# Block sums of the second output matrix formed from the float32 weights, one group's x sums moved to VectorE, and another order of the last output products

## The chip, the cores and the metric

One core of a Trainium2 chip runs the whole program. The metric is the device time of one execution in microseconds, the median of several runs. The engines are called as in the profile: PE (TensorE matmuls), PEld (its weight loads), DVE (VectorE), ACT (ScalarE), POOL (GpSimd), SP (SyncE, whose queue issues most DMAs).

## The reference

Attention with a relative bias over 4 x 8 heads of 576 x 64, then two feed-forward layers over 2304 tokens of 512 features. The change concerns the second layer:

```python
def _moe2_ref(x, w_gate, w_val, w_out):        # x 2304 x 512, d_ff 1536
    gate = 1.0 / (1.0 + np.exp(-(x @ w_gate)))
    val = x @ w_val
    return (gate * val @ w_out).astype(np.float32)
```

## The kernel before

Every float32 operand is split into two f16 parts, high and low, and a product is three f16 matmuls (high by high, high by low, low by high). The weights are decoded from their raw words (`decode`, L186), scaled and split in place: `w2f[mat]` (L1157) holds matrix `mat` (0 gate, 1 value, 2 output) as float32 and, after `w2_split` (L1179), as f16 pairs over the same memory (`w2h16`).

The second layer works on 18 tiles of 128 tokens in five groups of 4, 2, 4, 4 and 4 tiles (`sizes`). Groups 0 and 1 use plain products: `gate_val` (L1398) for gate and value, `second_out` (L1627) for the output. Groups 2 to 4 use a scheme of seven block products in place of eight for each 2 x 2 block product. This scheme needs sums of blocks on both sides:

- `w2_sums` (L1309) forms them for gate and value weights, on DVE with copies by ACT, into tiles `w2s`. There is one set for each of three parts `jc` of the 1536 inner features.
- `x2_sums` (L1338) forms x's sums of group 2 into tiles `x2s0` to `x2s3`, which have one buffer each. For groups 3 and 4, `next_sums` (L1424) forms x's sums one half `t` at a time in the tile `xx` (one buffer), stores them in DRAM (`xt_d`), and `load_sums` (L1455) loads them again.
- `out_sums` (L1483) forms the output matrix's sums from the f16 pairs of `w2h16[2]`: ten additions, three copies and three subtractions per `jc`, into `w3s`. For `jc` 0 and 1 DVE adds and ACT copies; for `jc` 2 POOL does both. `out_first` (L1497) forms the remaining sum, in place of the block b12, with four DVE operations and one ACT copy per `jc`. All of this runs when group 2 begins: `out_sums` for 0, 2, 1 and `out_first(0)` ahead of the loop at L1686, the other two `out_first` behind the first `gate7` of group 2.

`gate7` (L1514) makes 14 products of 12 matmuls for one `jc` (seven for the gate, seven for the value, by `seven`, L1381) and from them seven f16 pieces `ap`. Its float32 results take ten tiles of the ring `fr`. `out7` (L1594) makes the seven products of the output for one `jc` into four accumulators `c11`, `c12`, `c21`, `c22`; `out_last` (L1565) does it for the last `jc` of the last group and stores the blocks. Products go to eight PSUM buffers `prod`. `add` (L1300) is an operation by DVE and `padd` (L1440) one by POOL.

The loop over g = 2, 3, 4 has this order: `gate7(0)`, then x's sums for the next group, `gate7(1)`, `out7(0)`, `gate7(2)`, `load_sums`, `out7(1)`, `out7(2)` or `out_last`. The sums of group 3 are halved: t = 0 by DVE, t = 1 by POOL; both halves of group 4 are POOL's.

The order of instructions on each engine is set ahead of the run by a scheduler that goes by priority (the order of the program text, unless raised) and simulated readiness; `tc.issue_after(i)` puts what follows behind the instruction `i`. The weight work of the second layer is a list of small steps, `units` (L1223 to L1230), each with a count; `take(n)` (L1233) hands out n counts of them between the steps of attention's end and of `gate_val` for group 0 (5 per step for j below 8, then 7). Each engine and each DMA queue works in its order.

Of the kernel before, what the change touches and what calls it, by code (L numbers as in the profile page):

```python
# [102 lines left out]
def attn_moe_kernel(  # L103
# [19 lines left out]
    x2_d = dram.tile([18, 128, 4, 2, 128], F16, name="x2_d")  # L123
    xt_d = dram.tile([2, 2, 128, 2, 4, 2, 128], F16, name="xt_d")
# [592 lines left out]
    def split_w(w, s_, hi, lo, tmp, scaler=None, sub=None):  # L717
# [5 lines left out]
        (sub or pool).tensor_tensor(out=lo, in0=tmp, in1=hi, op=ALU.subtract)  # L723
# [498 lines left out]

    steps = [(m, jc) for jc in range(3) for m in range(2)]  # L1223
# [4 lines left out]
    units += decs(2, 0) + decs(2, 1) + decs(2, 2)  # L1228
    units += [(1, lambda: urgent(w2_scale_out))]
    units += [(1, lambda jc=jc, c=c: w2_split(2, jc, c)) for jc in range(3) for c in range(4)]  # L1230
    given = [0, 0]
# [208 lines left out]
    def padd(out_, a, b, op=ALU.add):  # L1440
        glob["pool"] = pool.tensor_tensor(out=out_, in0=a, in1=b, op=op)  # L1441

# [37 lines left out]
    def phigh(x, dst):  # L1480
        pool.tensor_scalar(out=dst(0), in0=x, scalar1=1.0, scalar2=None, op0=ALU.mult)

    def out_sums(jc, plus, top, tmp):  # L1483
        b11, b21, b12, b22 = out_blocks(jc)
        st_ = w3_p.tile([128, 3, 2, 2, 256], F16, name=f"w3s{jc}")

        def part(n):
            return lambda l, kk=None: st_[:, n, l] if kk is None else st_[:, n, l, kk]
        t2, t3, t4 = (part(n) for n in range(3))
        u, x, y, v = (tmp(n) for n in range(4))  # L1490
        tsums(u, x, y, v, b11, b21, b12, b22, plus)
        for f, dst_ in ((x, t2), (y, t3), (v, t4)):
            top(f, dst_)
            plus(dst_(1), f, dst_(0), ALU.subtract)
        osum[jc] = dict(b11=b11, b21=b21, b22=b22, t1=b12, t2=t2, t3=t3, t4=t4)

    def out_first(jc, plus, top):  # L1497
        w = osum[jc]
        u, v = ctile(0), ctile(3)
        plus(u, w["t1"](0), w["b11"](0), ALU.subtract)  # L1500
        plus(v, w["t1"](1), w["b11"](1), ALU.subtract)
        plus(u, u, v)
        top(u, w["t1"])
        plus(w["t1"](1), u, w["t1"](0), ALU.subtract)
# [45 lines left out]
    def put(g, th, e, c, tts):  # L1550
        o = slice(256 * e, 256 * e + 256)
        for tt in tts:
            tl = tiles[first[g] + 2 * th + tt]
            if tl[0] == "D":
                _, bp, qd, b, r = tl
                r0 = (2 * bp + b) * S + 256 * qd
                sp.dma_start(out=out[r0:r0 + 256, o].rearrange("(p r) m -> r p m", r=2)[r], in_=c[:, tt])
# [128 lines left out]
    for g in range(2, 5):  # L1686
        p0 = gate7(0, xs_)
        if g == 2:
            out_first(1, add, high)
            out_first(2, add, high)  # L1690
# [83 lines left out]
```

## Time and profile before

| | |
|---|---|
| median of three runs | 1057.43 us (1053.62 to 1063.36) |
| profiled execution, its own time | 1061.63 us |
| its span in the trace | 1059.8 us |
| busy, PE / PEld / DVE / ACT / POOL | 894.4 / 669.8 / 817.9 / 673.4 / 565.6 us |

The trace is of one execution on the chip; its times count from the span's start. A line such as L1301 can be that of a helper (`add`), so tiles say more than lines. PE's ends are modelled, so a piece of twelve matmuls reads 1.47 us where the next starts after 1.31. An engine's wait is put down to the last thing that it waited for.

### The profile page before, as it was taken

The numbers are of one execution on the slowest core, as the hardware profiler recorded it, in microseconds if no ns is written. First come the engines' busy times: TensorE is split into PE (matmuls) and PEld (weight loads), VectorE is DVE, ScalarE is ACT, GpSimd is POOL, SyncE is SP. The second block draws the span as 40 slices with busy tenths as digits, with TensorE's granted clock in tenths as the row PEclk, the third lists the DMA queues.
The fourth block names the chain that finished last, engine by engine and source line by source line (L and its number), as shares of the span: only waits on it lengthen the run. The fifth ranks groups of instructions, "written<-read, shape, count | busy, mean of one in ns | idle before, by whom it ended". The sixth has DMA issues, their size and how long they took to land. (4 is left out here: it accounts for less than half of the span.)

```text
span 1059.8 us, 25088 instructions
## 1 busy us (share of the span) xinstructions
PE 894.4 (84%) x9944; PEld 669.8 (63%) x9944; DVE 817.9 (77%) x1568; ACT 673.4 (64%) x1337; POOL 565.6 (53%) x514
## 2 busy tenths in 40 slices
PE   2646665678888799999998789999997889999997
PEld 2524454455666666677685465455766778888886
DVE  6879899786666766667568877589999966877877
ACT  4789886758677787888868976864333433443432
POOL 3357556565665556546642577230063575786346
PEclk9756565689999899999999989999999999999999
DMA  7878999899999999899878335010010131013001
GB/s 223 283 243 209 236 249 243 219 215 197 192 184 199 173 200 185 169 226 196 160 179 308 128 130 199 1 40 31 11 40 1 41 103 49 2 62 106 5 2 40
DMA packets 263046, 150.42 MB, mean 142 GB/s; under 512 B 216976, under 2 KB 237968, under 8 KB 262928
## 3 DMA queue, kind: packets, MB, share of 16 engines
q1 hardware_dynamic: 259632, 145.67, 57.1%
q0 software_dynamic: 2048, 1.58, 0.6%
q8 instruction: 78, 1.28, 0.5%
q10 hardware_dynamic: 1248, 1.57, 0.4%
q14 instruction: 40, 0.33, 0.1%
HBM read 84.03 MB, written 22.28 MB: 100 GB/s over the span
## 5 line engine op out<-in xcount | busy, mean ns | idle before, releaser
L617 POOL TENSOR_TENSOR p<-p,p 128x1024 f16<-128x1024 f32 x72 | 158.4, 2200 | 124.4 <-ACT p L616 84.1
L605 ACT ACTIVATE p<-p,m,sc 128x576 f32<-128x576 f32 x144 | 123.9, 863 | 2.4
L1301 DVE TENSOR_TENSOR fr<-prod,fr 128x512 f32<-128x512 f32 x144 | 95.4, 685 | 29.8 <-ACT fr L1385 15.6
L598 DVE CUSTOM_DVE_ANT_0 p<-score,gk 128x576 f32<-128x576 f32 x144 | 102.9, 750 | 11.0 <-PE score L580 7.1
L847 PE MATMUL x2ps<-lt,w1f 128*128 128x128 f16 x1728 | 108.1, 223 | 3.4 <-ACT lt L835 1.9
L847 PEld LDWEIGHTS <-w1f 128*128 128x128 f16 x1728 | 103.4, 100 | 4.0 <-issue 1.8
L1413 PE MATMUL s_ps<-xb,w2f 128*128 128x512 f16 (+1 forms) x576 | 99.3, 330 | 6.0 <-DVE fr L1419 4.8
L641 PE MATMUL xps<-gk,pt 128*128 128x64 f16 (+1 forms) x2240 | 86.8, 202 | 12.4 <-DMA pt<-p 10.7
L1377 PEld LDWEIGHTS <-w2f 128*128 128x128 f16 x864 | 85.5, 99 | 17.9 <-issue 7.1
L1441 POOL TENSOR_TENSOR ap<-fr,ap 128x512 f16<-128x512 f32 x45 | 59.0, 1322 | 69.7 <-ACT ap L1510 69.7
L641 PEld LDWEIGHTS <-pt 128*128 128x128 f16 (+1 forms) x2240 | 81.8, 106 | 22.7 <-DMA pt<-p 13.1
L464 PEld LDWEIGHTS <-mask 128*128 128x128 f16 (+1 forms) x1312 | 61.8, 118 | 53.9 <-issue 24.3
L1510 ACT ACTIVATE ap<-fr 128x512 f16<-128x512 f32 x63 | 38.9, 628 | 81.4 <-DVE fr L1521 46.1
L1413 PEld LDWEIGHTS <-w2f 128*128 128x128 f16 x576 | 56.4, 99 | 48.1 <-issue 10.3
L790 PE MATMUL hps<-w1f,xt 128*128 128x512 f16 x312 | 78.5, 399 | 5.7 <-DVE gk L263 3.0
L1542 PEld LDWEIGHTS <-ap 128*128 128x128 f16 x756 | 74.0, 98 | 8.6
L1377 PEld LDWEIGHTS <-w2s 128*128 128x128 f16 x648 | 64.6, 100 | 19.2 <-issue 10.5
L575 PE MATMUL score<-gk,qt 64*128 64x512 f16 x384 | 59.6, 416 | 17.8 <-DVE m L598 9.3
L464 PE MATMUL bp<-rhs,mask 128*128 128x64 f16 (+1 forms) x960 | 49.4, 219 | 28.7 <-DVE gb L490 11.3
L790 PEld LDWEIGHTS <-xt 128*128 128x128 f16 x384 | 37.8, 101 | 48.5 <-issue 13.5
L616 ACT ACTIVATE p<-p 128x1152 f16<-128x1152 f32 x54 | 62.4, 1158 | 9.1 <-DMA pt<-p 7.0
L1377 PE MATMUL prod<-x2s,w2s 128*128 128x256 f16 x432 | 55.6, 280 | 8.7 <-ACT fr L1385 8.7
(244 smaller groups left out, 2139.2 us busy)
## 6 DMA issues: line engine op xcount, KB each, us to landing
gk<-bias_d SPq DMA_DIRECT2D x24, 576.0 KB
wraw<-in_moe_w_out_dram SPq DMA_DIRECT2D x20, 512.0 KB
sraw<-in_q_dram SPq DMA_DIRECT2D x12, 384.0 KB
sraw<-in_k_dram SPq DMA_DIRECT2D x12, 384.0 KB
sraw<-in_v_dram SPq DMA_DIRECT2D x12, 384.0 KB
bias_d<-gk SPq DMA_DIRECT2D x8, 576.0 KB
qraw<-in_q_dram SPq DMA_DIRECT2D x64, 64.0 KB
kv<-in_k_dram SPq DMA_DIRECT2D x32, 128.0 KB
```

The costliest lines, as they stand in the source:

```text
L464: pe.matmul(big[0:np_, jj // 8, o:o + 64], lhsT, rhs[i].rearrange("p c h g -> p (c h g)"), start=(i == 0), stop=(i == 1),)
L598: dve.tensor_tensor_reduce(out=pp[:, hh], in0=score[:, 960 * hh:960 * hh + S], in1=bi, scale=1.0, scalar=-3.0e38, op0=ALU.add, op1=ALU.max ...
L605: act.activation(out=pp[:, hh], in_=pp[:, hh], func=ACTF.Exp, bias=m[:, 2 + hh:3 + hh], scale=col(C), accum_out=sm[:, c + hh:c + hh + 1])
L616: act.activation(out=hi, in_=pp, func=ACTF.Copy)
L617: pool.tensor_tensor(out=p16[:, :, 640:1152], in0=view(pp, 0, [[640, 2], [1, 512]]), in1=view(p16, 0, [[1280, 2], [1, 512]]), op=ALU.subtract)
L641: pe.matmul(o, a, b_, start=(n == 0), stop=(n == len(seq) - 1))
L790: pe.matmul(h, xt[:, xl, kk, off:off + 128], win16[:, 2 * kk + n, wl], start=(kk == 0 and xl == 0 and wl == 0), stop=(kk == 3 and xl == 1),)
L847: pe.matmul(ps[:, dc], wout16[:, f, wl, 128 * dc:128 * dc + 128], lt[:, ll, f], start=(n == 0), stop=(n == 23))
L1301: glob["dve"] = dve.tensor_tensor(out=out_, in0=a, in1=b, op=op)
L1377: pe.matmul(p[:, jf, 0:nn], w(wl, kk, jf), x(xl, kk), start=(m == 0), stop=(m == 5))
L1413: pe.matmul(ps[:, 0:n], w[:, 4 * (j // 4) + c, wl, o:o + 128], xx[:, 0:n, c, xl, :], start=(m == 0), stop=(m == 11))
L1542: pe.matmul(p[:, tt], a[:, al, kk, 128 * tt:128 * tt + 128], w(wl, kk), start=(m == 0), stop=(m == 5))
```

## The change

The sums of the output matrix are formed from the float32 weights as soon as these are decoded, before the in-place split overwrites them: four float32 subtractions by POOL per `jc` (`out_adds`), into temporaries that lie in the tiles of the `w2s` sums for `jc` 1 and 2. Behind the last split, ACT scales and rounds them, POOL forms the low parts (`out_split`), and SP stores the pairs in DRAM (`to_d`), by way of the tiles `x2s0` to `x2s3`. When group 2 begins, `out_sums` loads them, three sums into `w3s` and one over the block b12. `out_first` and `phigh` are gone. Both halves of x's sums of group 3 are DVE's. `out_last` makes its products in another order, adds with DVE where POOL did twice, and its stores alternate between SP and ACT.

```diff
@@ -121,6 +121,7 @@
     dram = enter(ctx, "scratch", 1, space=DRAM)
     bias_d = dram.tile([5, 128, H, 640], F32, name="bias_d")
     x2_d = dram.tile([18, 128, 4, 2, 128], F16, name="x2_d")
+    to_d = dram.tile([3, 128, 4, 2, 2, 256], F16, name="to_d")
     xt_d = dram.tile([2, 2, 128, 2, 4, 2, 128], F16, name="xt_d")
 
     const = enter(ctx, "const")
@@ -720,7 +721,7 @@
         else:
             pool.tensor_scalar(out=tmp, in0=w, scalar1=s_, scalar2=0.0, op0=ALU.mult, op1=ALU.add)
         act.activation(out=hi, in_=tmp, func=ACTF.Copy)
-        (sub or pool).tensor_tensor(out=lo, in0=tmp, in1=hi, op=ALU.subtract)
+        glob["split"] = (sub or pool).tensor_tensor(out=lo, in0=tmp, in1=hi, op=ALU.subtract)
 
     def behind(f):
         with tc.issue_after(glob["qk"].ins):
@@ -1220,14 +1221,46 @@
     def scale(m, jc):
         return [(1, lambda: urgent(lambda: (w2_scale_gate, w2_scale_val)[m](jc)))]
 
+    def padd(out_, a, b, op=ALU.add):
+        glob["pool"] = pool.tensor_tensor(out=out_, in0=a, in1=b, op=op)
+
+    tmps = {}
+
+    def out_adds(jc):
+        if jc == 0:
+            four = [sw_p.tile([128, 3, 2, 256], F32, name=f"w2s{m}{n}") for n in (1, 2) for m in range(2)]
+            tmps.update((n, four[n // 3][:, n % 3]) for n in range(12))
+        b11, b21, b12, b22 = (w2f[2][:, 4 * jc + 2 * kh:4 * jc + 2 * kh + 2, 256 * e:256 * e + 256]
+                              for kh, e in ((0, 0), (1, 0), (0, 1), (1, 1)))
+        u, x, y, v = (tmps[4 * jc + n] for n in range(4))
+        padd(u, b12, b11, ALU.subtract)
+        padd(x, b22, u, ALU.subtract)
+        padd(y, b22, b12, ALU.subtract)
+        padd(v, b21, x, ALU.subtract)
+
+    def behind_splits(jc):
+        with tc.issue_after(glob["split"].ins):
+            out_split(jc)
+
+    def out_split(jc):
+        for n in range(4):
+            f = tmps[4 * jc + n]
+            d = xs_p.tile([128, 2, 2, 256], F16, name=f"x2s{n}")
+            act.activation(out=f, in_=f, func=ACTF.Copy, scale=sw[:, jc, S_O:S_O + 1])
+            act.activation(out=d[:, 0], in_=f, func=ACTF.Copy)
+            padd(d[:, 1], f, d[:, 0], ALU.subtract)
+            sp.dma_start(out=to_d[jc, :, n], in_=d)
+
     steps = [(m, jc) for jc in range(3) for m in range(2)]
     units = decs(*steps[0])
     for n, (m, jc) in enumerate(steps):
         units += decs(*steps[n + 1]) if n < 5 else []
         units += scale(m, jc) + splits(m, jc)
-    units += decs(2, 0) + decs(2, 1) + decs(2, 2)
+    for jc in range(3):
+        units += decs(2, jc) + [(1, lambda jc=jc: out_adds(jc))]
     units += [(1, lambda: urgent(w2_scale_out))]
     units += [(1, lambda jc=jc, c=c: w2_split(2, jc, c)) for jc in range(3) for c in range(4)]
+    units += [(1, lambda jc=jc: behind_splits(jc)) for jc in range(3)]
     given = [0, 0]
 
     def take(n):
@@ -1437,9 +1470,6 @@
             plus(dst_(1), f, dst_(0), ALU.subtract)
         sp.dma_start(out=xt_d[g - 3, t], in_=xx)
 
-    def padd(out_, a, b, op=ALU.add):
-        glob["pool"] = pool.tensor_tensor(out=out_, in0=a, in1=b, op=op)
-
     def tsums(u, x, y, v, b11, b21, b12, b22, plus):
         plus(u, b12(0), b11(0), ALU.subtract)
         plus(v, b12(1), b11(1), ALU.subtract)
@@ -1477,31 +1507,16 @@
     def ctile(n):
         return c_p.tile([128, 2, 256], F32, name=f"c{n}")
 
-    def phigh(x, dst):
-        pool.tensor_scalar(out=dst(0), in0=x, scalar1=1.0, scalar2=None, op0=ALU.mult)
-
-    def out_sums(jc, plus, top, tmp):
+    def out_sums(jc):
         b11, b21, b12, b22 = out_blocks(jc)
         st_ = w3_p.tile([128, 3, 2, 2, 256], F16, name=f"w3s{jc}")
+        sp.dma_start(out=st_, in_=to_d[jc, :, 1:4])
+        for l in range(2):
+            sp.dma_start(out=b12(l), in_=to_d[jc, :, 0, l])
 
         def part(n):
             return lambda l, kk=None: st_[:, n, l] if kk is None else st_[:, n, l, kk]
-        t2, t3, t4 = (part(n) for n in range(3))
-        u, x, y, v = (tmp(n) for n in range(4))
-        tsums(u, x, y, v, b11, b21, b12, b22, plus)
-        for f, dst_ in ((x, t2), (y, t3), (v, t4)):
-            top(f, dst_)
-            plus(dst_(1), f, dst_(0), ALU.subtract)
-        osum[jc] = dict(b11=b11, b21=b21, b22=b22, t1=b12, t2=t2, t3=t3, t4=t4)
-
-    def out_first(jc, plus, top):
-        w = osum[jc]
-        u, v = ctile(0), ctile(3)
-        plus(u, w["t1"](0), w["b11"](0), ALU.subtract)
-        plus(v, w["t1"](1), w["b11"](1), ALU.subtract)
-        plus(u, u, v)
-        top(u, w["t1"])
-        plus(w["t1"](1), u, w["t1"](0), ALU.subtract)
+        osum[jc] = dict(b11=b11, b21=b21, b22=b22, t1=b12, t2=part(0), t3=part(1), t4=part(2))
 
     osum = {}
 
@@ -1547,18 +1562,18 @@
         act.activation(out=c, in_=c, func=ACTF.Copy, scale=col(CO))
         put(g, th, e, c, range(2))
 
-    def put(g, th, e, c, tts):
+    def put(g, th, e, c, tts, queues=(sp, sp)):
         o = slice(256 * e, 256 * e + 256)
         for tt in tts:
             tl = tiles[first[g] + 2 * th + tt]
             if tl[0] == "D":
                 _, bp, qd, b, r = tl
                 r0 = (2 * bp + b) * S + 256 * qd
-                sp.dma_start(out=out[r0:r0 + 256, o].rearrange("(p r) m -> r p m", r=2)[r], in_=c[:, tt])
+                queues[tt].dma_start(out=out[r0:r0 + 256, o].rearrange("(p r) m -> r p m", r=2)[r], in_=c[:, tt])
             else:
                 for par in range(2):
                     r0 = (2 * tl[1] + par) * S + 512
-                    sp.dma_start(out=out[r0:r0 + 64, o], in_=c[64 * par:64 * par + 64, tt])
+                    queues[tt].dma_start(out=out[r0:r0 + 64, o], in_=c[64 * par:64 * par + 64, tt])
 
     cs = {}
 
@@ -1572,19 +1587,19 @@
             for lo, hi in halves:
                 dve.scalar_tensor_tensor(out=c_[:, lo:hi], in0=p[:, lo:hi], scalar=col(CO), in1=c_[:, lo:hi],
                                          op0=ALU.mult, op1=ALU.add)
-                put(g, th, e, c_, range(lo, hi))
+                put(g, th, e, c_, range(lo, hi), (sp, act))
 
         act.activation(out=a, in_=oproduct(ps["a", 1, 1], w["b11"]), func=ACTF.Copy)
-        padd(c11, c11, a)
+        add(b, oproduct(ps["s", 2], w["t2"]), a)
+        add(c11, c11, a)
+        add(c, oproduct(ps["s", 3], w["t3"]), b)
+        add(c22, c22, c)
         p2 = oproduct(ps["a", 1, 2], w["b21"])
         done_(c11, p2, 0, 0)
-        add(b, oproduct(ps["s", 2], w["t2"]), a)
-        padd(c12, c12, b)
-        add(c, oproduct(ps["s", 3], w["t3"]), b)
-        add(c22, c22, c)
+        add(c21, c21, c)
+        add(c12, c12, b)
         p5 = oproduct(ps["s", 1], w["t1"])
         add(c12, p5, c12)
-        add(c21, c21, c)
         done_(c22, p5, 1, 1)
         p4 = oproduct(ps["a", 2, 2], w["t4"])
         done_(c21, p4, 1, 0)
@@ -1679,23 +1694,18 @@
     ts_p = enter(ctx, "ts", 1)
     w3_p = enter(ctx, "w3", 1)
     c_p = enter(ctx, "c", 1)
-    out_sums(0, add, high, ctile)
-    out_sums(2, padd, phigh, lambda n: f32t())
-    out_sums(1, add, high, ctile)
-    out_first(0, add, high)
+    for jc in range(3):
+        out_sums(jc)
     for g in range(2, 5):
         p0 = gate7(0, xs_)
         if g == 2:
-            out_first(1, add, high)
-            out_first(2, add, high)
-        if g < 4:
-            if g == 2:
-                with tc.issue_after(glob["dve"].ins):
-                    next_sums(3, 0, add)
+            with tc.issue_after(glob["dve"].ins):
+                for t in range(2):
+                    next_sums(3, t, add)
+        if g == 3:
             with tc.issue_after(glob["pool"].ins):
-                if g == 3:
-                    next_sums(4, 0, padd)
-                next_sums(g + 1, 1, padd)
+                for t in range(2):
+                    next_sums(4, t, padd)
         p1 = gate7(1, xs_)
         out7(g, 0, p0)
         p2 = gate7(2, xs_)
```

## Rows read from the trace of the kernel before

**Rows 1.** Windows, all engines: stretch and length, busy us (instructions), clock, DMA share, GB/s.
```profile
664.42:696.30 31.88, 31.48 (x139) 14.02 (x139) 14.69 (x33) 27.66 (x48) 10.42 (x10) 0.95 0.00 1
696.30:720.17 23.87, 23.66 (x158) 15.24 (x156) 23.84 (x38) 11.05 (x20) 4.13 (x3) 1.00 0.12 45
720.17:764.80 44.63, 44.63 (x270) 26.12 (x268) 44.56 (x80) 17.79 (x34) 0.00 (x0) 1.00 0.06 25
764.80:783.49 18.69, 17.03 (x114) 10.86 (x112) 17.75 (x28) 7.09 (x15) 6.14 (x5) 1.00 0.09 29
783.49:835.27 51.78, 40.41 (x336) 34.17 (x336) 51.58 (x69) 16.85 (x29) 27.51 (x19) 0.93 0.07 21
835.27:868.33 33.06, 29.50 (x255) 25.53 (x252) 22.36 (x32) 12.46 (x23) 24.88 (x25) 0.95 0.12 42
868.33:886.83 18.50, 18.50 (x172) 16.58 (x170) 14.61 (x20) 5.38 (x9) 14.09 (x11) 1.00 0.35 113
886.83:969.36 82.53, 82.53 (x759) 73.98 (x757) 62.21 (x82) 32.09 (x57) 59.82 (x60) 1.00 0.16 55
```

**Rows 2.** Timeline of PE: start, length, line, tile, count [idle before, releaser].
```profile
664.42 7.03 PE L1413 MATMUL s_ps<-xb,w2f 128*128 128x512 f16 x24 [4.17 <-DVE fr L1419]
...
720.17 24.98 PE L1634 MATMUL ops<-w2f,gv 128*128 128x512 f16 x115
...
783.49 1.47 PE L1377 MATMUL prod<-xb,w2f 128*128 128x256 f16 x12 [1.14 <-ACT ob L1638]
...
822.63 2.72 PE L1377 MATMUL prod<-x2s,w2s 128*128 128x256 f16 x12 [4.29 <-ACT fr L1385]
...
858.81 1.56 PE L1377 MATMUL prod<-x2s,w2s 128*128 128x256 f16 x12 [2.62 <-ACT fr L1385]
```

**Rows 3.** Chain of waits, in order of time, one piece of it.
```profile
886.83 36.68 PE prod L1377 x336
```

**Rows 4.** Windows by tile (`c` twice, then `ts`): DVE, ACT, POOL busy.
```profile
764.80:783.49 18.69, 11.81 (x16) 1.67 (x3) 0.00 (x0) 1.00 0.09 29
783.49:835.27 51.78, 23.03 (x23) 3.78 (x6) 0.00 (x0) 0.93 0.07 21
...
783.49:868.33 84.84, 8.56 (x14) 3.32 (x8) 10.90 (x14) 0.94 0.09 29
```

**Rows 5.** Waits of the DMA queue of SP, 640 to 1060: total, times, longest.
```profile
SPq L1428 <- DMA xt_d<-xx: 5.2, 2, 3.0
```

**Rows 6.** Groups of instructions, 640 to 1060: line, engine, shapes, count, busy, mean ns.
```profile
L723 POOL TENSOR_TENSOR w2f<-w2tmp,w2f 128x512 f16<-128x512 f32 x17 | 22.2, 1311 | 26.4 <-ACT w2f L722 25.9
L1441 POOL TENSOR_TENSOR fr<-fr 128x512 f32<-128x512 f32 x20 | 28.4, 1419 | 11.3 <-DVE fr L1301 11.2
L719 ACT ACTIVATE w2tmp<-w2f,sw 128x512 f32<-128x512 f32 x12 | 8.5, 714 | 1.0 <-DVE sw L1206 0.9
L722 ACT ACTIVATE w2f<-w2tmp 128x512 f16<-128x512 f32 x21 | 12.9, 623 | 4.1 <-POOL w2tmp L721 1.9 <-DVE lt L836 1.9
```

**Rows 7.** Timelines of DVE and ACT, 696 to 765.
```profile
696.31 4.79 DVE L1301 TENSOR_TENSOR fs<-w2f 128x512 f32<-128x512 f16 x3
...
734.50 1.88 DVE L1301 TENSOR_TENSOR fs<-w2f 128x512 f32<-128x512 f16 x3
...
764.18 0.68 DVE L1301 TENSOR_TENSOR w2s<-fs,w2s 128x512 f16<-128x512 f32 x1
...
717.89 0.63 ACT L1304 ACTIVATE x2s<-fs 128x512 f16<-128x512 f32 x1
```

**Rows 8.** Timeline of POOL, PE, SP's queue and DVE at the end.
```profile
1045.40 6.18 POOL L1441 TENSOR_TENSOR c<-c,fr 128x512 f32<-128x512 f32 x5 [0.33 <-DVE fr L1301]
...
1050.42 1.47 PE L1542 MATMUL prod<-w2f,ap 128*128 128x256 f16 x12
...
1051.92 5.25 SPq L1557 DMA_DIRECT2D out_dram<-c  x8
...
1053.61 2.18 DVE L1573 SCALAR_TENSOR_TENSOR c<-prod,sc,c 128x512 f32<-128x512 f32 x4
```

## Prediction

> **What bounds the kernel now.** I read the stretches of the second half first [rows 1]. From 664 to 783 us PE is busy in almost every microsecond (31.5 of 31.9, 23.7 of 23.9, all of 44.6, 17.0 of 18.7): the plain gate, value and output products of groups 0 and 1 set the pace there, although DVE is just as full from 696 to 765 with the block sums of the gate and value matrices. From 783.49 to 868.33 the third group (g = 2) runs and PE drops to 40.4 of 51.8 and 29.5 of 33.1; from 886.83 on PE is full again (82.53 of 82.53 for the whole of g = 3) and stays so to 1051.9. So there is one hole, in the third group, and a tail of 7.9 us after PE's last product.
>
> The hole's size comes from PE's order of time [rows 2]. From 783.49 to 868.33 PE runs 49 products of 12 matmuls (three `gate7` of 14 and one `out7` of 7). The chain of waits shows what a product costs when nothing stops it: 336 matmuls, 28 products, in 36.68 us, 1.31 us each [rows 3]. 49 of those are 64.2 us; the stretch takes 84.84. The hole is 20.6 us. Two of its waits stand in rows 2: 4.29 us for ACT's copy of a product (it waits for a free `fr` tile, that is, for DVE and POOL to finish the gates before), and 2.62 us of the same kind, whose copy waited for POOL's `c` additions. What fills DVE in the first 51.8 us (51.58 busy) is seen by tile [rows 4]: 11.8 us of `c` operations before 783.49 and 23.0 us after it are the sums of the output matrix (`out_sums`, `out_first`), of DVE's 73.9 in the two stretches of the hole; the other 50.9 hold the 14 operations for x's next sums (8.56 us). POOL does the other half of x's sums there, 10.9 us.
>
> **The change, part by part.** *Third group.* The `out_sums` of jc 0 and 1 and the three `out_first` leave DVE: 34.8 us of [rows 4], 23.0 of them in the hole. POOL loses `out_sums(2)` (16 operations, mostly ahead of the hole) and the 14 operations for t = 1 of x's sums, 10.9 us; DVE takes these 14, at the price of the other half, 8.56 us. DVE's work between 783.49 and 868.33 becomes 51.58 + 22.36 - 23.03 + 8.56 = 59.5 us [rows 1, 4], under PE's 64.2. So PE is the bound again, narrowly. What is late next: the two batches of x's sums. Each is issued behind DVE's last addition of a `gate7`, with precedence over the DVE work of the `gate7` that follows, so 8.56 us of DVE stand in front of the copies that free PSUM; eight product tiles are 8 x 1.31 = 10.5 us of cover, of which the end of a `gate7` already uses some. Bounds for what this leaves: 0, and 8.56 (the second batch wholly in the way, the first under the cover); the nearest row is the one wait of 4.29 us, in the `gate7` beside which the first batch ran [rows 2]. I take 4. The second batch waits besides for the store of the first and its own load, since tile `xx` has one buffer: SP's row shows 3.0 us for that wait [rows 5], and PE has `out7` then, with little DVE work. POOL's `c` additions lose the batch in front of them. Stage: 64.2 + 4 = 68.2, a gain of 16.6 us (bounds 12.1 and 20.6).
>
> *The loads in their place.* Nine DMAs, 3 x (768 + 2 x 128) KB = 3.1 MB, stand on SP ahead of the loads of `xx`. Their memory comes free with the last plain products, about 783. While x's sums were loaded, 868.33 to 886.83, 113 GB/s moved [rows 1]; at that rate the nine take 28 us, the first third 9.3. `out7(0)` needs the first third 28 products after 783.5, at 820: hidden under two `gate7`. If the cover were gone, the first third would cost 9.3 us.
>
> *The sums made early.* POOL gets 12 float32 additions; the nearest rows are 1.31 and 1.42 us [rows 6], so 15.8 to 17.0 us from the decodes of that matrix on. ACT gets 24 operations of 0.71 and 0.62 us, 16.1 us; POOL 12 subtractions of 1.31 us, 15.7 us; SP 12 stores of 256 KB. These follow the last split of the output matrix, which ends about 700.4 (POOL's 4.13 us after 696.30). POOL is idle from there to 764.8 and ACT is busy 11.1 of 23.9 and 17.8 of 44.6 us [rows 1]. So the room is there; the order is the question. Three waits are added: ACT's overwriting of the decoded weights waits for POOL's additions (POOL works 10.4 of 31.9 us in 664 to 696, so 16 fit); the temporaries lie in the tiles of the `w2s` sums for jc 1 and 2; the f16 pairs lie in `x2s0` to `x2s3`, one buffer each, so each round of four waits for the stores of the last, and `x2_sums(2)`, on ACT and then DVE, for the stores of the third. By ACT alone the three rounds take 16.1 us and end near 717, just as ACT's first write of `x2s` came in the trace (717.9 [rows 7]). Behind the waiting DVE operation stand the sums of jc 1 and 2 and the gate and value steps of group 1. PE has plain output products then as filler, 144 of 0.217 us, 31 us (115 took 24.98 [rows 2]), and the sums have slack: they end at 764.8 [rows 7] and PE takes them up at 783.5; the 11.8 us of `out_sums(0)` that followed them are gone.
>
> POOL's 12 subtractions fall beside these sums. Three sums with two SBUF inputs took 4.79 us while POOL ran and 1.88 us while it did not [rows 7, 1]: 0.97 us for each, 11.6 us for twelve. The sums then end at 776.4, still ahead of 783.5: cost 0, bounds -4.2 (the 4.17 us for which PE waits at 664 [rows 2], since the decodes now come a step later among the gates) and +9.3.
>
> The Trainium skill, page "SBUF — State Buffer", section "Who interferes with whom", speaks against this part: a VectorE instruction with two SBUF inputs and a GpSimd one that reads SBUF exclude each other for a whole instruction, and whoever starts first wins. The trace agrees (the three sums above). By that rule the loss is between 0 and a whole 1.31 us for each, 15.7 us, and the sums would end as late as 780.5, with 3 us of slack left instead of 7, which speaks for the last of the rivals.
>
> *The end.* PE's last product ends at 1051.89, the span at 1059.8 [rows 1, 8]. POOL's five `c` additions run from 1045.40 to 1051.58, and block c11, whose last product ended near 1045, is stored behind them; SP then issues eight stores in 5.25 us from 1051.92 on, and the span ends 2.6 us after the last of them. In the new order `c11` and `c12` are added by DVE and the stores alternate between SP and ACT, so three blocks are out before the last product. After it come two halves on DVE (4 take 2.18 us: 0.55 each), some 0.6 us of queue, an issue of 0.65 us and the 2.6 us: 1051.89 + 1.1 + 0.6 + 0.65 + 2.6 = 1056.8. Gain 3.0 us, bounds 0 (ACT's scalings stand behind its stores) and 4.
>
> **Sum.** 16.6 + 0 + 3.0 = 19.6 us. The profiled execution took 1061.63 us; 1042.0 remain. The median of the runs, 1057.43, lies 4.2 us below the profiled one, so I forecast 1038.
>
> **Rivals.** *DVE stays the bound of the third group.* In g = 3, where PE is full, DVE stands 20.3 of 82.53 us [rows 1], because each gate is a chain through ACT and POOL. If it stands as much here, 59.5 + 20.3 x 64.2 / 82.53 = 75.3 us, the gain is 9.5 + 3.0 and the time 1045. For it: DVE's margin is 4.7 us in 64. Against: those waits are for PE's products or end under the eight product tiles.
>
> *The front goes faster too.* PE's 4.17 us at 664 go, and the batches hide wholly: 1038 - 8 = 1030. For it: the decodes, at which ACT stood for a DMA, come later in its order. Against: POOL's additions come into the same stretch.
>
> *Slower: the early sums become one late chain.* If the POOL additions all stand in front of the splits (15.8 us), the three rounds go one store at a time (per round 1.33 + 1.31 + 3.0 + 3 x 1.33 = 9.6, so 28.9 for 16.1, 12.8 more), and POOL holds up DVE (11.6 us), the sums end 40.2 us later, 21.5 past 783.5. DVE's steps for group 1 stand in the same queue, and PE's own stage would end some 12.8 us later by the standing alone: together 34 us against the gain of 19.6, 1072. It decides when the delay passes 18.7 us of slack plus the gain, 38. For it: `x2s` with one buffer, and the lock. Against: POOL is busy for only a third of 664 to 696, and the pieces overlap.
>
> That the change does not do what it says is no rival: the DVE work that goes is in the rows.
>
> **How the numbers follow.** Forecast 0.56 (own range 1033 to 1043), DVE the bound 0.25, faster front 0.12, late chain 0.07. The measurement tells about 1% from no change: 1046.9 and 1068.0. Faster: 0.56 + 0.12 + somewhat under half of 0.25, 0.79; slower 0.07; the same 0.14. The range leaves out the late chain and the outermost of the others: 1030 to 1053.
>
> **What would show it.** Right: the 49 products of g = 2 take 66 to 70 us, with no wait over 4.5 us, and no DVE `c` operation from weights; `x2s` first written by x2_sums before 725; PE's first `gate7` still near 783; span end under 5.5 us after PE's last product. Wrong: PE waiting between 690 and 783, the first `gate7` later than 790, or DVE over 95% busy with PE waits through all of g = 2.

## Result and profile after

The changed kernel takes 1064.81 us (median of 20 runs, 1058.2 to 1067.53) where the kernel before takes 1056.38 (20 runs beside them): a ratio of 1.0072, 95% interval 1.0053 to 1.0091. The forecast was 1038 with a range of 1030 to 1053. Some 19 us of expected gain became a loss of 8.

Up to about 640 us every engine has the same instructions in the same order in both kernels, yet the traced execution of after reaches that point some 10 us earlier than that of before; single executions differ by as much. I therefore count from one common event, the pair of gate and value products of group 0 behind the last `x2ps` product (649.72 before, 639.88 after). From there to the third group's first product I call the **front**. Windows of after, same columns as [rows 1]; the first is the front, then the 49 products of g = 2, the rest of PE's products, and what follows PE's last one:

```profile
639.88:796.30 156.42, 134.56 (x725) 73.72 (x723) 121.93 (x170) 84.34 (x151) 64.34 (x43) 0.93 0.19 66
796.30:864.70 68.40, 64.51 (x588) 57.50 (x588) 57.79 (x87) 25.18 (x45) 22.81 (x17) 1.00 0.22 73
864.70:1049.59 184.89, 183.91 (x1682) 164.12 (x1679) 151.61 (x193) 68.74 (x117) 120.16 (x103) 1.00 0.11 37
1049.59:1056.40 6.81, 0.00 (x0) 0.00 (x0) 3.57 (x7) 1.70 (x3) 0.00 (x0) 0.87 0.44 154
```

The front of before, for comparison:

```profile
649.72:783.49 133.77, 127.32 (x725) 70.93 (x723) 110.21 (x185) 72.62 (x129) 28.80 (x24) 0.99 0.12 42
```

Before, the four stretches are 133.8, 84.84, 183.6 and 7.9 us. So the front grew by 22.6, the third group gained 16.4, the rest lost 1.3 and the end gained 1.1: +6.4 us, against +8 in the medians. The whole question lies in the front. PE ran the same 725 matmuls there, but stood idle for 21.9 us (156.42 - 134.56) where it had stood 6.5, and the matmuls took 134.56 instead of 127.32 us, at a granted clock of 0.93 instead of 0.99.

PE's waits of over 1 us in the front of after, from its timeline, and the first two waits inside the third group (behind 796.30):

```profile
655.02 7.03 PE L1446 MATMUL s_ps<-xb,w2f 128*128 128x512 f16 x24 [3.83 <-DVE fr L1452]
665.53 10.43 PE L1446 MATMUL s_ps<-xb,w2f 128*128 128x512 f16 x40 [3.48 <-DVE fr L1452]
711.67 2.78 PE L1446 MATMUL s_ps<-xb,w2f 128*128 128x256 f16 x24 [3.35 <-DVE fr L1452]
...
725.87 4.93 PE L1446 MATMUL s_ps<-xb,w2f 128*128 128x256 f16 x24 [5.36 <-DVE fr L1452]
765.46 8.22 PE L1446 MATMUL s_ps<-xb,w2f 128*128 128x256 f16 x48 [3.08 <-DVE fr L1452]
796.30 1.47 PE L1410 MATMUL prod<-xb,w2f 128*128 128x256 f16 x12 [1.14 <-ACT ob L1653]
851.55 1.47 PE L1410 MATMUL prod<-x2s,w2f 128*128 128x256 f16 x12 [2.69 <-DVE fr L1334]
854.22 1.47 PE L1410 MATMUL prod<-xb,w2s 128*128 128x256 f16 x12 [1.20 <-DVE fr L1334]
```

All waits of the front but the last name `fr` of L1452: the DVE step in `gate_val` that multiplies value by gate and so frees one of the two PSUM pairs, which the step after next needs. What the third wait held up (24 matmuls of 256 columns, 2.78 us) ran at a granted clock of 1.00; the same 24 behind the wait of 5.36 took 4.93, at 0.55. Why DVE was late, from the timelines of ACT, DVE and POOL of after:

```profile
679.67 7.44 ACT L1249 ACTIVATE w2s<-w2s,sw 128x512 f32<-128x512 f32 x12
687.02 1.13 ACT L723 ACTIVATE w2f<-w2tmp 128x512 f16<-128x512 f32 x2
688.06 2.18 ACT L1250 ACTIVATE x2s<-w2s 128x512 f16<-128x512 f32 x4
690.14 0.61 ACT L1315 ACTIVATE gv<-fr 128x512 f16<-128x512 f32 x1
...
690.78 0.69 DVE L1316 TENSOR_TENSOR gv<-fr,gv 128x512 f16<-128x512 f32 x1 [11.51 <-ACT gv L1315]
695.87 4.77 DVE L1334 TENSOR_TENSOR fs<-w2f 128x512 f32<-128x512 f16 x3
...
718.84 3.20 DVE L1334 TENSOR_TENSOR fs<-xb 128x512 f32<-128x512 f16 x2
...
662.62 5.06 POOL L1225 TENSOR_TENSOR w2s<-w2f,w2s 128x512 f32<-128x512 f32 x3
...
716.80 1.56 POOL L724 TENSOR_TENSOR w2f<-w2tmp,w2f 128x512 f16<-128x512 f32 x1 [1.81 <-ACT w2f L723]
718.33 6.27 POOL L1225 TENSOR_TENSOR x2s<-w2s,x2s 128x512 f16<-128x512 f32 x4
727.05 6.01 POOL L1225 TENSOR_TENSOR x2s<-w2s,x2s 128x512 f16<-128x512 f32 x4 [2.45 <-ACT x2s L1250]
735.83 6.22 POOL L1225 TENSOR_TENSOR x2s<-w2s,x2s 128x512 f16<-128x512 f32 x4 [2.77 <-ACT x2s L1250]
```

ACT has all twelve scalings of the early sums (L1249) in one block, ahead of group 0's gate copies; DVE stands 11.51 us for such a copy. `tc.issue_after` on the last split holds back POOL's low parts alone, since that split is POOL's instruction. The block also pushes the splits back: POOL's last one (L724) ends at 718.36, 78.5 us into the front, where it ended 50.8 us into it before. Then POOL's twelve low parts run from 718.33 to 742 beside DVE's sums, and the two-input sums there take 1.60 us each (3.20 for two) instead of 0.68. By these rows the first of DVE's sums of gate and value weights starts 56.0 us into the front (46.6 before), and the last `w2s` sum ends 141.9 us into it (115.1 before).

At the end of the kernel, timelines of PE, DVE and SP's queue:

```profile
1048.12 1.47 PE L1557 MATMUL prod<-w2f,ap 128*128 128x256 f16 x12
...
1048.51 1.29 DVE L1334 TENSOR_TENSOR c<-c,fr 128x512 f32<-128x512 f32 x2
1049.72 0.74 DVE L1588 SCALAR_TENSOR_TENSOR c<-prod,sc,c 128x512 f32<-128x512 f32 x1
1050.38 0.68 DVE L1334 TENSOR_TENSOR c<-prod,c 128x512 f32<-128x512 f32 x1
1050.98 2.18 DVE L1588 SCALAR_TENSOR_TENSOR c<-prod,sc,c 128x512 f32<-128x512 f32 x4
...
1050.49 2.74 SPq L1572 DMA_DIRECT2D out_dram<-c  x4
```

The order laid out for DVE has the additions to c22, c21 and c12 ahead of the first scaled addition (L1588), so every store still leaves behind the end of PE's last product, as in [rows 8].

### The profile page after: what moved, and what is told of

It reads as the page before. It is cut to its first block, busy times and chain, and to the rows that moved or that the text cites. A ratio compares the mean times of both kernels' runs of the same rounds, so it can differ in the third digit from the quotient of the medians.

```text
span 1056.4 us, 25115 instructions
## 1 busy us (share of the span) xinstructions
PE 890.7 (84%) x9944; PEld 664.0 (63%) x9944; DVE 819.7 (78%) x1546; ACT 681.5 (65%) x1352; POOL 573.7 (54%) x506
## 5 line engine op out<-in xcount | busy, mean ns | idle before, releaser
L1446 PE MATMUL s_ps<-xb,w2f 128*128 128x512 f16 (+1 forms) x576 | 105.5, 345 | 21.8 <-DVE fr L1452 20.6
L848 PE MATMUL x2ps<-lt,w1f 128*128 128x128 f16 x1728 | 105.0, 220 | 3.2 <-ACT lt L836 2.0
L848 PEld LDWEIGHTS <-w1f 128*128 128x128 f16 x1728 | 100.2, 99 | 3.5 <-issue 1.1
L1446 PEld LDWEIGHTS <-w2f 128*128 128x128 f16 x576 | 59.2, 103 | 68.2 <-issue 28.9
L642 PE MATMUL xps<-gk,pt 128*128 128x64 f16 (+1 forms) x2240 | 87.3, 202 | 14.5 <-DMA pt<-p 12.5
L642 PEld LDWEIGHTS <-pt 128*128 128x128 f16 (+1 forms) x2240 | 82.0, 107 | 24.2 <-DMA pt<-p 14.7
L465 PEld LDWEIGHTS <-mask 128*128 128x128 f16 (+1 forms) x1312 | 59.6, 115 | 52.4 <-issue 23.8
L791 PE MATMUL hps<-w1f,xt 128*128 128x512 f16 x312 | 75.8, 389 | 5.0 <-DVE gk L264 2.3
L791 PEld LDWEIGHTS <-xt 128*128 128x128 f16 x384 | 37.5, 101 | 47.1 <-issue 11.8
L604 ACT ACTIVATE m<-m,sc 128x1 f32<-128x1 f32 x144 | 39.3, 286 | 36.2 <-DVE m L599 35.9
```

Source lines behind the costliest of these rows:

```text
L465: pe.matmul(big[0:np_, jj // 8, o:o + 64], lhsT, rhs[i].rearrange("p c h g -> p (c h g)"), start=(i == 0), stop=(i == 1),)
L642: pe.matmul(o, a, b_, start=(n == 0), stop=(n == len(seq) - 1))
L791: pe.matmul(h, xt[:, xl, kk, off:off + 128], win16[:, 2 * kk + n, wl], start=(kk == 0 and xl == 0 and wl == 0), stop=(kk == 3 and xl == 1),)
L848: pe.matmul(ps[:, dc], wout16[:, f, wl, 128 * dc:128 * dc + 128], lt[:, ll, f], start=(n == 0), stop=(n == 23))
L1446: pe.matmul(ps[:, 0:n], w[:, 4 * (j // 4) + c, wl, o:o + 128], xx[:, 0:n, c, xl, :], start=(m == 0), stop=(m == 11))
```

## Experiments

All times are compared with the kernel before, run beside them; ratios have 95% intervals. "First" and "last" are the start of DVE's first operation for the sums of the gate and value weights and the end of the last, counted like the front; "rest" goes from the third group's first product to PE's last, "end" from there to the span's end.

| kernel | ratio to before | front | first | last | rest | end |
|---|---|---|---|---|---|---|
| before | | 133.8 | 46.6 | 115.1 | 268.4 | 7.9 |
| after | 1.0072 [1.0053, 1.0091] | 156.4 | 56.0 | 141.9 | 253.3 | 6.8 |
| e1, no early sums | 0.9843 [0.9813, 0.9873] | 132.2 | 46.1 | 114.6 | 253.3 | 7.0 |
| e2, copies held | 1.0071 [1.0045, 1.0097] | 153.5 | 51.6 | 137.2 | 254.9 | 6.8 |
| e3, no low parts by POOL | 1.0000 [0.9981, 1.0019] | 146.0 | 60.8 | 136.8 | 253.3 | 6.8 |
| e4, no additions by POOL | 1.0056 [1.0033, 1.0080] | 151.3 | 49.8 | 136.3 | 253.3 | 7.3 |
| e5, neither | 0.9977 [0.9950, 1.0004] | 143.4 | 58.2 | 134.2 | 254.9 | 6.8 |
| e6, additions and stores | 0.9936 [0.9914, 0.9958] | 139.7 | 51.4 | 122.0 | 253.3 | 6.8 |
| e12, POOL beside | 0.9933 [0.9911, 0.9955] | 143.1 | 44.5 | 124.6 | 253.3 | 7.0 |
| e11, more DVE work | 0.9839 [0.9807, 0.9871] | 135.0 | 47.5 | 130.7 | 253.3 | 7.0 |
| e8, end alone | 1.0011 [0.9985, 1.0038] | 132.2 | 45.0 | 113.6 | 266.7 | 7.1 |
| e7, float32 in DRAM | 0.9956 [0.9933, 0.9980] | 139.5 | 47.4 | 118.0 | 256.2 | 7.4 |
| e9, the same, held | 0.9943 [0.9920, 0.9965] | 137.5 | 48.7 | 119.3 | 257.9 | 7.1 |
| e10, additions by DVE | 0.9923 [0.9895, 0.9952] | 133.7 | 48.5 | 116.0 | 257.9 | 6.8 |

**e1: the change without the early sums.** `out_adds` and `out_split` are left out, and the loads take rows of x of the same size.

```diff
-        units += decs(2, jc) + [(1, lambda jc=jc: out_adds(jc))]
+        units += decs(2, jc)
-    units += [(1, lambda jc=jc: behind_splits(jc)) for jc in range(3)]
...
-        sp.dma_start(out=st_, in_=to_d[jc, :, 1:4])
+        sp.dma_start(out=st_..., in_=x2_d[4 * jc + 1:4 * jc + 4]...)
```

> Leaves out the early sums altogether (no additions, copies, low parts or stores); the loads at the start of group 2 take the same number of bytes from x's stored tiles instead. If the whole loss lies in the stretch ahead of group 2 (22.6 us between the same two points of PE's work in the two traces, 649.72 to 783.49 before and 639.88 to 796.30 after), the time is 1064.8 - 22 = 1042 to 1044, a ratio to the kernel before of 0.986 to 0.989, with PE's wait-free stretch ahead of group 2 back at 134 us. If the loss lies elsewhere (the loads, DVE in group 2, the end), it stays above 1052, ratio over 0.995.

Measured 1039.31 us, front 132.2. The whole loss sits in forming the sums early (24.2 us of front); all that the change takes away is gained, 17 us where 19.6 were forecast.

**e2: ACT's scalings held behind the last split too.**

```diff
-        act.activation(out=hi, in_=tmp, func=ACTF.Copy)
+        glob["hi"] = act.activation(out=hi, in_=tmp, func=ACTF.Copy)
...
-        with tc.issue_after(glob["split"].ins):
+        with tc.issue_after(glob["split"].ins), tc.issue_after(glob["hi"].ins):
```

> ACT's 24 operations for the early sums are held behind ACT's last copy of the splits (the hold in the change holds POOL's instructions only). If the block of 16 such operations ahead of the splits and of group 0's gate steps costs the 9 us by which the sums of the gate and value matrices start later, the time is 1055 to 1057, ratio 0.998 to 1.001, and the splits end some 18 us earlier. If the collision of POOL and DVE carries nearly all of the loss, 1061 to 1065, ratio 1.005 to 1.008.

Measured 1065.01 us, no gain. The sums begin 4.4 us earlier into the front and ACT's last copy of the splits comes 16.8 us earlier, but the block of twelve now stands at 704.50, among ACT's copies for these sums, and their stretch is as long as in after (85.6 us from first to last, against 85.9). Moving the block moves the wait; the time lies at the upper end of the second case.

**e3 and e4: parts of POOL's work taken out.** e3 has ACT write both halves in one wide operation and leaves out POOL's subtractions of the low parts; e4 fills the temporaries with four memsets instead of the twelve subtractions.

```diff
-            act.activation(out=d[:, 0], in_=f, func=ACTF.Copy)
-            padd(d[:, 1], f, d[:, 0], ALU.subtract)
+            act.activation(out=d, in_=f[:, None].to_broadcast([128, 2, 2, 256]), func=ACTF.Copy)
```

```diff
+            for t in four:
+                pool.memset(t, 1.0)
...
-        padd(u, b12, b11, ALU.subtract)
...
-        padd(v, b21, x, ALU.subtract)
```

> POOL's 12 low-part subtractions are left out; ACT writes the high part twice in one wider operation each (5 us more on ACT). If POOL beside DVE is what lengthens DVE's sums (83.8 us from first to last against 68.5), 12 to 15 us come back: 1050 to 1053, ratio 0.994 to 0.997, and operations of DVE with two SBUF inputs read 0.68 us throughout after 718. If the late start set by ACT's order carries the loss, 1061 to 1064.

> POOL's 12 float32 additions are left out; four memsets fill the temporaries, and the scalings work on constants. If the additions cost PE its two waits of 3.83 and 3.48 us near 655 and 666, 3 to 6 us come back: 1059 to 1062, ratio 1.002 to 1.005. If they only fill idle time of POOL, 1063 to 1066, ratio 1.006 to 1.009.

Measured 1056.61 and 1062.92 us; the fronts are 10.4 and 5.1 us shorter than in after. Both times fall between their two cases, and the interval of e4 overlaps that of after, so what the additions cost shows in the traces alone: of PE's two waits near 655 and 666 the first falls from 3.83 to 1.24 us, the second from 3.48 to 3.12. In e3 the sums still take 76.0 us from first to last (e1: 68.5), and operations with two SBUF inputs do not read 0.68 us throughout, for POOL's splits, pushed back by ACT's block, now run beside them until 733.02 (timelines of POOL and DVE of e3):

```profile
731.73 1.29 POOL L724 TENSOR_TENSOR w2f<-w2tmp,w2f 128x512 f16<-128x512 f32 x1 [3.35 <-ACT w2f L723]
...
731.93 1.64 DVE L1333 TENSOR_TENSOR fs<-xb,fs 128x512 f32<-128x512 f16 x1
```

**e5 and e6: what is left from either side.** e5 joins e3 and e4. e6 keeps the additions and stores the float32 sums at once; ACT's work and the low parts are left out, and the loads take rows of x as in e1.

```diff
-            d = xs_p.tile([128, 2, 2, 256], F16, name=f"x2s{n}")
-            act.activation(out=f, in_=f, func=ACTF.Copy, scale=sw[:, jc, S_O:S_O + 1])
-            act.activation(out=d[:, 0], in_=f, func=ACTF.Copy)
-            padd(d[:, 1], f, d[:, 0], ALU.subtract)
-            sp.dma_start(out=to_d[jc, :, n], in_=d)
+            sp.dma_start(out=to_f[jc, :, n], in_=f)
```

> GpSimd gets none of the early sums' work: its 12 adds become 4 memsets of the destinations and its 12 lower halves go (ScalarE writes both halves with one wide operation); ScalarE's 12 scalings, 12 copies, the x2s slots and the 12 stores stay. By single changes the adds cost about 2 us and the lower halves about 8. If these two costs only add up: 1054.7 us (1064.8 - 8.2 - 1.9), and ScalarE's 24 instructions with the slots cost the remaining 15. If the two hide each other (GpSimd late either way, VectorE slowed either way): 1040 to 1046, front near 134 us.

> The 12 adds on GpSimd stay, and 12 stores of the float32 sums to DRAM right behind them; no scaling, no copy, no lower half, no x2s slot. The loads of the last stage take rows of x instead, as in the run without the early sums, so the sums themselves are computed and not used. If ScalarE's 24 instructions, the slots and the lower halves carry the loss: the time without the early sums plus 2 for the adds, 1041 us, front 132 to 135. If the adds' place in GpSimd's order and the stores on SP's queue carry it: 1050 or more, front over 142.

Measured 1054.37 and 1049.58 us: e5 is what the two costs give if they add up; e6 lies between its two cases, near the dearer one (front 139.7, where 142 were named). Step by step the front goes from 156.4 (after) by 5.1 without the additions, 7.9 more without the low parts, and 11.2 more without ACT's 24 instructions, the slots and the stores. The last figure is somewhat high, since ACT's twelve copies are wide in e3 and e5 (11.8 us in place of 6.9). From the other side, additions and stores alone cost 7.5, more than the 2 that I gave them; without the low parts, the additions cost only 2.6 (e3 against e5). No single part carries it. ACT's block shows best in e5, whose POOL does no arithmetic for the early sums (timelines of ACT and DVE):

```profile
685.08 7.44 ACT L1244 ACTIVATE w2s<-w2s,sw 128x512 f32<-128x512 f32 x12
...
697.95 1.29 DVE L1446 SCALAR_TENSOR_TENSOR fr<-s_ps,fr 128x512 f32<-128x512 f32 x2 [13.27 <-ACT fr L1445]
```

**e11 and e12: does slack hide a delay of DVE?** This is the step on which the forecast of 0 for the front stood, so it is tried alone, on e1. e11 repeats one subtraction 20 times among the sums; e12 puts twelve subtractions on POOL behind the last split, which nobody waits for.

```diff
-        low(y, s4)
+        for _ in range(21 if (mat, jc) == (0, 0) else 1):
+            low(y, s4)
```

```diff
+    def beside():
+        t = sw_p.tile([128, 3, 2, 256], F32, name="w2s12")
+        pool.memset(t, 1.0)
+        with tc.issue_after(glob["split"].ins):
+            for n in range(12):
+                padd(t[:, 0], t[:, 1], t[:, 2], ALU.subtract)
```

> The kernel without the early sums, with one subtraction of the first set of gate sums made 21 times instead of once: 20 more VectorE operations of 0.68 us, 13.6 us, among the sums, and known to the scheduler when it lays out the order (it spreads them and puts the gate and value steps of group 1 between). Forecast's reading (the sums have 18.7 us of slack and PE has filler): the sums end 13.6 us later, the front grows by 0 to 2 us, time 1039 to 1042. If VectorE's work ahead of group 1's steps goes to PE in full, known or not: front 142 to 146, time 1049 to 1053.

> The kernel without the early sums, with 12 GpSimd subtractions behind the last split, SBUF to SBUF, which nobody waits for, in the place of the lower halves: the collision alone, which the scheduler does not know of, with none of ScalarE's 24 instructions and no late start. If the lengthening of the sums goes to PE: 12 x 0.97 us, sums 80 instead of 68.5 us long, front 140 to 144, time 1047 to 1051. If the slack hides it: front 132 to 134, time 1039 to 1041.

Measured 1041.9 and 1051.4 us (ratios 0.9839 and 0.9933). In e11 the last sum ends 16.1 us later than in e1, and the front grows by 2.8: the scheduler knows of the 20 operations, spreads them from 710 us on, and lays PE's plain output products otherwise between its steps. In e12 DVE has e1's order among the sums, the last sum ends 10.0 us later, and the front grows by 10.9. Timelines of POOL, DVE and PE of e12:

```profile
693.89 20.10 POOL L1225 TENSOR_TENSOR w2s<-w2s 128x512 f32<-128x512 f32 x12
...
697.75 0.68 DVE L1434 SCALAR_TENSOR_TENSOR fr<-s_ps,fr 128x512 f32<-128x512 f32 x1
...
706.12 3.41 DVE L1316 TENSOR_TENSOR fs<-w2f 128x512 f32<-128x512 f16 x2
709.45 1.74 DVE L1316 TENSOR_TENSOR fs<-fs,w2f 128x512 f32<-128x512 f32 x1
711.12 1.75 DVE L1316 TENSOR_TENSOR fs<-fs 128x512 f32<-128x512 f32 x1
712.79 0.68 DVE L1434 SCALAR_TENSOR_TENSOR fr<-s_ps,fr 128x512 f32<-128x512 f32 x1
...
713.52 5.28 PE L1428 MATMUL s_ps<-xb,w2f 128*128 128x256 f16 x24 [9.23 <-DVE fr L1434]
```

This is the mechanism in one view: while POOL works (1.67 us for each), each DVE operation with two SBUF inputs takes POOL's time instead of 0.68 us; between group 0's last two gate and value steps (L1434, 697.75 and 712.79) stand nine of them, eight sums and one low part of `gv`, and PE's second step of group 1 waits 9.23 us for the latter of the two. In e11 that step starts without a wait (703.59), and the next waits 0.22 us.

**e8: the end alone, on the kernel before.** Functions `put` and `out_last` of after, nothing else.

> The kernel before with the changed order and queues of the last outputs alone. The forecast had -3.0 us for it; the changed kernel's trace shows 6.8 us behind the last product instead of 7.9, that is -1.1. Forecast: 1053.3 us; trace of the changed kernel: 1055.2. No change outside the last 30 us.

Measured 1057.33 us, ratio 1.0011: no difference that can be told. Its end is 7.1 us by the trace. Its front, with the instructions of before, is 132.2 us; so 1.6 us of a front is the spread between executions.

**e7, e9, e10: a version that keeps part of the gain.** The sums go to DRAM as float32 straight from the additions, and are scaled and split in the third group, each by one ACT and one DVE instruction. What is computed is the reference's function.

```diff
+        for n in range(4):
+            sp.dma_start(out=to_f[jc, :, n], in_=tmps[4 * jc + n])
...
+        for n, dst in enumerate((b12, part(0), part(1), part(2))):
+            f = ctile(n)
+            sp.dma_start(out=f, in_=to_f[jc, :, n])
+            act.activation(out=dst(0), in_=f, func=ACTF.Copy, scale=s_)
+            dve.scalar_tensor_tensor(out=dst(1), in0=f, scalar=s_, in1=dst(0), op0=ALU.mult, op1=ALU.subtract)
```

> The sums are kept in DRAM as float32, unscaled, straight from GpSimd's adds, and scaled and split after the third group has begun: 12 loads, 12 ScalarE instructions (scale and round in one), 12 VectorE instructions (scale and subtract in one). The function computed is that of the reference. If the loss of the change sits in scaling and splitting inside the front: front near 134 us, and the third group gets back 12 x 0.68 to 12 x 1.64 us of VectorE (8 to 20 us), part of it beside idle VectorE: 1045 to 1053, below both kernels. If the adds and stores already cost the front 10 us or more: 1055 to 1066.

Measured 1052.46 us, below both kernels and within what was expected. The first product of the third group waits for it (timelines of PE and ACT of e7): ACT stands at the loads ahead of the evacuation `ob` of group 1, and the product starts when that ends.

```profile
783.25 2.72 PE L1398 MATMUL prod<-xb,w2f 128*128 128x256 f16 x12 [4.55 <-DMA c<-to_f]
...
775.37 0.72 ACT L1508 ACTIVATE w2f<-c,sw 128x512 f16<-128x512 f32 x1 [3.60 <-DMA c<-to_f]
...
782.53 0.67 ACT L1644 ACTIVATE ob<-ops,sc 128x512 f32<-128x512 f32 x1
```

e9 holds DVE's part of the scaling and splitting behind the third group's first additions (ACT's scalings for `jc` 0 still run ahead, from 781.42 on), and at the end the additions to c22, c21 and c12 behind the first scaled addition; e10 has the twelve early additions on DVE besides (`add` for `padd`).

```diff
+            with tc.issue_after(glob["dve"].ins):
+                for jc in range(3):
+                    if jc:
+                        out_sums(jc)
+                    todo[jc]()
...
+        with tc.issue_after(glob["done"].ins):
+            add(c22, c22, c)
+            add(c21, c21, c)
+            add(c12, c12, b)
```

> The float32 version with its scaling and splitting held behind the first additions of the third group on ScalarE and VectorE, and in the last outputs the three additions of sums held behind the first scaled addition, so that its stores leave first. If the 4.55 us wait at the third group's first product came from ScalarE standing at the loads ahead of the evacuation of the second group: that wait goes back to about 1 us, front 136, and with 1 us less at the end 1046 to 1049 (the run without the hold: 1052.5). If the loads have to be waited for anyway, later in the stage: 1051 to 1054.

> The same with the 12 adds on VectorE in place of GpSimd. If what the adds cost (first sum of the gate and value weights 51.4 instead of 46.1 us into the front with adds and stores alone) is GpSimd's order, where they stand ahead of the scalings that ScalarE's first splits wait for: first sum near 47, front about 5 us shorter than in the run beside it, 1041 to 1045. If VectorE is as full there as behind it: 12 x 0.68 = 8.2 us come in its place and the time is the same or up to 3 us more.

Measured 1051.38 and 1048.97 us. In e9 the wait is gone (1.23 us), as in its first case, but the time is that of the second; e10's lies between its two. In both the rest takes 4.6 us more than in after: PE's waits in it add up to 8.3 us in e10 and to 4.9 in after. The longest of e10's eight, 2.15 us at 815.49 for a copy by ACT, comes behind ACT's own wait of 4.37 us for the loads of `jc` 1. Four more follow each other in the output products of g = 2 (0.65, 0.72, 1.00 and 0.82 us, for `c` and `fr`); that the 24 added instructions cause these too is not shown. So part of what was taken out of the front is paid there. With the additions on DVE the front is 3.8 us shorter than e9's, and only 1.5 longer than e1's, with the same twelve stores in it as in e6, so the stores cost little. e10 is the fastest that computes the reference's function, 0.77% below the kernel before. The end of e9, timelines of PE, SP's queue and DVE:

```profile
1042.47 1.47 PE L1552 MATMUL prod<-w2f,ap 128*128 128x256 f16 x12
...
1042.56 4.75 SPq L1567 DMA_DIRECT2D out_dram<-c  x4
...
1041.80 0.74 DVE L1583 SCALAR_TENSOR_TENSOR c<-prod,sc,c 128x512 f32<-128x512 f32 x1
1042.45 1.89 DVE L1322 TENSOR_TENSOR c<-c,fr 128x512 f32<-128x512 f32 x3
1044.44 0.69 DVE L1322 TENSOR_TENSOR c<-prod,c 128x512 f32<-128x512 f32 x1
1045.05 2.18 DVE L1583 SCALAR_TENSOR_TENSOR c<-prod,sc,c 128x512 f32<-128x512 f32 x4
```

Here the first store leaves before the last product ends, and the end is still 7.1 us: the last store waits for DVE's queue (until 1047.23), not for the stores ahead of it.

## Why the prediction was wrong

**Third group: right.** Forecast 68.2 us for the 49 products, measured 68.40. DVE is busy 57.79 us (forecast 59.5), PE waits 2.69 and 1.20 us (forecast 4 in all), behind the second batch of x's sums. The rival "DVE stays the bound" fell with it. The loads in their place are hidden, as forecast: PE's first product waits 1.14 us for `ob` as before, and neither wait inside the 49 products names a load.

**The sums made early: wrong, and with it the forecast.** The step that failed is the sentence that "the sums have slack" and that PE has plain output products as filler, from which the cost was taken as 0 with +9.3 as the upper bound (for which no working is given; the only 9.3 worked out is that of the loads). It measured 24.2 us, after against e1. For POOL's twelve low parts alone the delay was right: 11.6 us were forecast for the lock between POOL and DVE, and e12 measured just that (the sums took 80.1 us from first to last instead of 68.5). But a delay of the sums is not taken out of the 18.7 us behind the last of them. The last gate and value steps of group 0 and those of group 1 stand among the sums in DVE's fixed order, and PE pays at them. In after, the last sum ended 26.8 us later than in before: 9.4 from the late start, 17.4 from longer sums, beside which POOL's late splits ran as well as the low parts (e3 keeps 7.5 us of lengthening without low parts). Taken out of the slack, 26.8 us would have cost 8.1. PE lost 22.6, and from the last sum to the third group there were still 14.5 us of the 18.6. e11 shows that DVE work of 13.6 us among the sums can be nearly hidden (2.8 us) when the order is laid out with it; e12, that a lengthening of 11.6 which the order does not know is paid almost in full. The two differ in place as well, since e12's delay falls ahead of e11's operations, on a stretch where PE has 14 plain output products as filler instead of 110; what each of these differences counts for is not separated.

**ACT's part was misplaced.** I had its operations follow the last split, set 16.1 us of them against ACT's idle share and took them to end near 717, where `x2_sums` first writes. It was not the sum but the place: the twelve scalings stand ahead of group 0's gate copies, DVE stood 11.51 us for one of these, the splits ended late, and the sums began 9.4 us late.

**The clock was left out.** Behind some of the waits PE ran at the lower of its two levels, 1.2 instead of 2.4 GHz: behind e12's wait the granted clock was 0.51 and the 24 matmuls took 5.28 us instead of 2.78 (windows of e12, the wait and what followed):

```profile
704.00:713.50 9.50, 0.28 (x2) 0.00 (x1) 9.50 (x8) 1.23 (x3) 9.05 (x6) 0.74 0.00 0
713.52:718.80 5.28, 5.28 (x25) 3.75 (x25) 5.28 (x9) 1.88 (x5) 0.47 (x1) 0.51 0.00 0
```

In after's front this is 7.2 us of the 22.6 (134.56 - 127.32 busy). Not every wait was followed by it: behind 3.35 us at 711.67 the granted clock was 1.00, behind 3.08 us at 765.46 it was 0.65.

**The end: mis-sized.** Forecast -3.0, traces -1.1, e8 nothing measurable. The term at fault is "two halves on DVE", 1.1 us: after PE's last product DVE still has 3.57 us of work, since the scaled additions queue behind the plain ones. The rest of that sum holds: from DVE's last half to the span's end after takes 3.2 us, forecast 3.85.

**The rivals.** "The early sums become one late chain" named the place, the lock and the group 1 steps. Its price was too high (1072) and its condition wrong: it was to decide only past 38 us of delay, with the slack used up first. A chance of 0.07 came from that condition. Two of the three signs set for a failure were there: PE waits between 690 and 783, and a first `gate7` later than 790 (796.30). Of the signs set for being right, those of the third group were there, but `x2_sums` first wrote `x2s` at 741.73, not before 725, and the end took 6.8 us, not under 5.5.

The Trainium skill, page "SBUF — State Buffer", section "Who interferes with whom", has the rule that I weighed and priced at most at one POOL instruction for each collision. e12 agrees with it: DVE and POOL alternate at 1.67 us, while the DVE instruction that takes one input from PSUM keeps 0.68. What the rule can't tell is who stands behind the loser.

**Still open.** Why the scheduler put ACT's block where it did is in no trace. How the 24.2 us divide among the parts depends on the order in which they are taken away (the low parts are 7.9 to 10.9 us, the additions 2.6 to 7.5, the upper figure with the stores).

## What to carry to other kernels

Slack behind the last of a chain need not cover a delay inside it: here, what lengthened instructions in a fixed order, a collision or a late copy, was paid at the next instruction of another chain in that queue. So look for who stands between, not for who ends last. Before moving work to an idle engine, list whose instructions it stands ahead of there, and which engine's operations it collides with. Moving only what has few operations (raw sums to DRAM, scaling at the place of use) kept part of the gain (0.4 to 0.8% of the 1.6% that e1 shows).

## What was not expected of the hardware

Twelve POOL subtractions that nobody waited for cost 10.9 us of front (e12), nearly their own lengthening of DVE (11.6), and most of it in a single wait of PE. And such a wait can cost more than its length: behind those 9.23 us, the next 24 matmuls took 2.5 us more.
